# Gating a batch's loads behind the transpose ahead, reordering start-up PSUM banks, and turning q one step sooner

## The chip, the cores and the metric

The kernel runs on one core of one Trainium2 chip. The core has TensorE (PE, matmuls), VectorE (DVE), ScalarE (ACT), GpSimd (POOL) and SyncE (SP), each with its own stream of instructions, executed in order. SP and POOL issue most of the DMA transfers here. Matmul results go to PSUM, eight banks of 2 KB in each of 128 partitions; all else lives in SBUF. The metric is device time in microseconds for one execution; lower is better.

## The reference

A linear attention without softmax feeds a two-layer MLP. Eight batches, eight heads, 576 rows, head size 64; the MLP has 4608 tokens, width 512 and hidden width 2048. Its input is the attention's output, with the heads side by side.

```python
def _attn_ref(q, k, v, g_norm):
    kv = np.einsum('bhsd,bhse->bhde', k, v)
    out = np.einsum('bhsd,bhde->bhse', q, kv)
    rms = np.sqrt(np.mean(out * out, axis=-1, keepdims=True) + 1e-06)
    return (out / rms * g_norm).astype(np.float32)

def _moe_ref(x, w_in, w_out):
    h = x @ w_in
    g = np.where(h > 0.0, h, alpha * (np.exp(np.minimum(h, 0.0)) - 1.0))   # alpha = 1
    return (g @ w_out).astype(np.float32)
```

Inputs and output are float32; the kernel computes its matmuls in bfloat16.

## The kernel before

**Groups.** The 4608 tokens are worked in nine groups of 512. Group T below 8 holds the first 512 rows of batch T; group 8 holds the last 64 rows of all eight batches. Batch and group share their number. A group's MLP has eight steps. A step `mm1(T, i)` makes two 128-wide blocks of the hidden layer, transposed, with eight matmuls of 128x512 (line 399); ScalarE takes the exponential from PSUM (line 411), VectorE makes min(e, 1) - 1 (line 420) and the maximum of that and h (line 428), which gives `gT`. With `relu` ScalarE also writes relu(h) to SBUF (line 415) and VectorE adds that instead of reading PSUM. The second product `mm2` (line 444) gathers 16 matmuls for each of four output blocks `o_ps`, copied by ScalarE (line 457) and stored by SP (line 466). From group 2 on the second product of group T-1 runs between the steps of group T, and so does the attention of batch T+1.

**Attention of one batch.** Its pieces are, in order: `kv` (72 small matmuls, line 177, then ScalarE's copies into the block-diagonal `bd_kv`, line 356); `se` for two halves (line 208, from qT and bd_kv, then a square on ScalarE); sums, the reciprocal root, and VectorE's scaling into `xs` (line 242); and the turn of xs into `xT`. For batches 1 and 2 TensorE turns xs. From batch 3 on SP does it in two DMA transposes (`xd0`, `xd1`, line 327), and VectorE scales each half by g (`xg0`, `xg1`, line 334). In group T these pieces stand after steps 0 (kv), 1 (se0), 2 (xd0), 3 (se1), 4 (xd1), 5 (xg0) and 6 (xg1). Step 0 of the next group needs xT complete.

**Loads.** `fetch(b)` has POOL issue the loads of q, k and v of batch b, which cast float32 to bfloat16 on the way (lines 104 and 118), and then unpack q with four copies (line 151); the last of these stands behind a 1-element copy that waits for v (`gate<-v_pk`, line 125). When q is unpacked, SP issues a DMA transpose into `qT` (`qd`, line 265), in program order after the group's xT transposes and stores. `landed` is another 1-element POOL copy; it reads qT of a batch, and so holds back all that stands behind it on POOL until that transpose has landed. Before the change it stands ahead of the loads of batches 3 and 4 alone. k, v and q have two buffers each.

**Start.** Group 0 has its own code. Batch 0's q is turned by TensorE; kv, se, squares, means (a matmul with a matrix of 1/64), logarithm, exponential and scaling follow for the four head pairs c = 0 to 3 (`kv_first`, `se_first`, `square_first`, `mean_first`, `log_first`, `exp_first`, `scale_first`). They use banks by name; a name gets its place in PSUM in the order of first use, behind the two banks of `kv`. After `head.close()` the pools of the main part take the same eight banks: `at` the first two, then two h_ps tiles of two banks (`ps_m1`), then two single banks (`ps_m2`). A new tile waits for the last reader of what lay there. Idle matmuls on zeros (line 525) fill gaps.

**q of batch 1.** Batch 1's q is turned by TensorE, 32 transposes (`q_t`, line 188) into the tile `at`, during group 0; two copies bring it to SBUF (lines 258 and 259). kv of batch 1 uses `at` again, after step 7 of group 0, and the first quarter of the second product follows it.

Of the kernel before, what the change touches and what calls it, by code (L numbers as in the profile page):

```python
# [9 lines left out]
BF16 = mybir.dt.bfloat16  # L10
# [6 lines left out]
def kernel(  # L17
# [13 lines left out]
    nc = tc.nc  # L31
# [109 lines left out]
    def load_w_out(s):  # L141
        fs = slice(4 * s, 4 * s + 4)
        nc.gpsimd.dma_start(
            out=w_out_sb[:, fs, :], in_=moe_w_out.rearrange("(c p) f -> p c f", p=P)[:, fs, :]
        )
# [21 lines left out]
    def at_tile(dtype):  # L167
        full = ps_at.tile([P, 1024], FP32, name="at", tag="at")
        return full if dtype == FP32 else full.bitcast(BF16)
# [15 lines left out]
    def q_t_single(q_pk, qt_ps, p):  # L185
        for j in range(J):
            for l in range(2):
                nc.tensor.transpose(
                    qt_ps[l * 64 : l * 64 + 64, p, j * P : j * P + P],
                    q_pk[:, 2 * p + l, j, :],  # L190
                    ident,
                )
# [56 lines left out]
    def attention(T):  # L249
        st = {}  # L250

        def q_t():
            qt_ps = at_tile(BF16).rearrange("p (r t) -> p r t", r=NPAIR)
            qT = attp.tile([P, NPAIR, G], BF16, name="qT", tag="qT")
            st["qT"] = lambda p, j: qT[:, p, j * P : j * P + P]
            for p in range(NPAIR):
                q_t_single(raw["q", T], qt_ps, p)
            nc.vector.tensor_copy(out=qT[:, 0:2, :], in_=qt_ps[:, 0:2, :])
            nc.scalar.copy(qT[:, 2:4, :], qt_ps[:, 2:4, :])

        def q_dma():
# [99 lines left out]
        def kv_part(u):  # L361
# [4 lines left out]
            return product  # L366

        pieces = {"kv": kv_all, "q": q_t, "qd": q_dma}
        pieces["landed"] = lambda: after(st["at"])
        for h in range(2):  # L370
# [12 lines left out]
    def mm1(T, i, cols=(slice(0, 512),), relu=False, spare=False):  # L383

        if i == 0:
            gT[T] = mlpg.tile([P, FC, G], BF16, name="gT", tag="gT")
        x = xT[T]
        if spare:
            h_ps = [ps_m2.tile([P, G], FP32, name="h_ps", tag="mm2") for _ in range(2)]
            parts = [(a, a + 1, h_ps[a].rearrange("p (a t) -> p a t", a=1)) for a in range(2)]  # L390
        else:
            both = ps_m1.tile([P, 2, G], FP32, name="h_ps", tag="mm1")
            h_ps = [both[:, a, :] for a in range(2)]
            parts = [(0, 2, both)]
        for cs in cols:
            for a in range(2):
                f = 2 * i + a
                for c in range(KC):
                    nc.tensor.matmul(  # L399
                        h_ps[a][:, cs],  # L400
                        lhsT=w_in_sb[:, c, f * P : f * P + P],
                        rhs=x(c, cs),
                        start=(c == 0),
                        stop=(c == KC - 1),
                    )
        return elu(T, i, parts, relu)
# [32 lines left out]
    def mm2(T, j, f0, f1, hold=False):  # L439

        if f0 == 0 and (T, j) not in o_ps:
            o_ps[T, j] = ps_m2.tile([P, DM], FP32, name="o_ps", tag="mm2")
        for f in range(f0, f1):
            nc.tensor.matmul(  # L444
                o_ps[T, j],
                lhsT=gT[T][:, f, j * P : j * P + P],
                rhs=w_out_sb[:, f, :],
                start=(f == 0),
                stop=(f == FC - 1),
            )  # L450
        if f1 == FC and not hold:
            mm2_out(T, j)
# [50 lines left out]
    for s in range(2):  # L503
# [7 lines left out]
        out=g_row,  # L511
        in_=bass.AP(tensor=g_norm.tensor, offset=g_norm.offset, ap=[[1, 1], [0, 2], [1, 64]]),
# [7 lines left out]
    def bank(n):  # L520
        return ps_head.tile([P, G], FP32, name=f"bank{n}", tag=f"bank{n}")

    def idle(ps, n):
        for _ in range(n):
            nc.tensor.matmul(ps, lhsT=zeros[:, 0:P], rhs=zeros, start=True, stop=True)

    kv_ps = ps_head.tile([P, 2, G], FP32, name="kv_ps", tag="kv")
    idle_ps, g_ps = bank(2), bank(3)
    qt_ps = [bank(n).bitcast(BF16).rearrange("p (r t) -> p r t", r=2) for n in (4, 5, 1)]
    idle(idle_ps, 9)  # L530
    q_st = q_tile(0)
    qT0 = attp.tile([P, NPAIR, G], BF16, name="qT", tag="qT")
# [15 lines left out]
    xT[0] = lambda c, cs: x0[:, c, cs]  # L548
    sq0 = [attp.tile([P, G], BF16, name="sq0", tag="sq0", bufs=4) for _ in range(KC)]
    r0 = [attp.tile([P, G], FP32, name="r0", tag="r0", bufs=4) for _ in range(KC)]  # L550
    mean0 = {}

    def kv_first(c):
        u, l = c // 2, c % 2
# [4 lines left out]
    def se_first(c):  # L559
        u, l = c // 2, c % 2  # L560
        ls = slice(l * 64, l * 64 + 64)
        for s in range(2):
            nc.tensor.matmul(
                se0[c][s * 64 : s * 64 + 64, :],
                lhsT=kv0[ls, u, s, :],
                rhs=qT0[ls, 2 * s + u, :],
                start=True,
                stop=True,
            )

    def square_first(c, eng):
        if eng is A:
            nc.scalar.activation(sq0[c], se0[c], AF.Square)
        else:
            nc.vector.tensor_copy(out=r0[c], in_=se0[c])
            nc.vector.tensor_tensor(out=sq0[c], in0=r0[c], in1=se0[c], op=ALU.mult)

    def mean_first(c):
        nc.tensor.matmul(mean0[c], lhsT=means, rhs=sq0[c], start=True, stop=True)

    def log_first(c):
        nc.scalar.activation(r0[c], mean0[c], AF.Ln, bias=eps_col)  # L582

    def exp_first(c):
        nc.scalar.activation(r0[c], r0[c], AF.Exp, scale=-0.5)  # L585

    def scale_first(c):
# [13 lines left out]
        start=True,  # L601
# [5 lines left out]
    square_first(0, A)  # L607
    kv_first(1)
    idle_ps = bank(4)
    for c in range(2):  # L610
        mean0[c] = bank(2 + c)
    mean_first(0)
    log_first(0)
    se_first(1)
# [14 lines left out]
    idle_ps = bank(2)  # L629
    idle(idle_ps, 1)  # L630
    mean_b = ps_head.tile([P, 2, G], FP32, name="mean_ps", tag="kv")
    mean0[2] = mean_b[:, 0, :]
    mean_first(2)
    log_first(2)
    exp_first(2)
    se_first(3)
    square_first(3, V)
    scale_first(1)
    scale_first(2)
# [14 lines left out]
    for c in range(KC):  # L654
        for f in (2, 3, 0, 1) if c == 0 else range(4):
# [4 lines left out]
                start=(c == 0),  # L660
                stop=(c == KC - 1),
            )
    at, ahead = attention(1), attention(2)
    for i in range(2):
        elu(0, i, [(0, 2, firsts[i])], i == 0)()
    for i in range(2, 8):
        mm1(0, i, relu=i in (2, 4, 7), spare=i in (3, 6))()
        if i in (3, 5):
            load_w_out(i // 2)
        if i == 6:  # L670
            at["q"]()
    for l in range(2):
        ls = slice(l * 64, l * 64 + 64)
        nc.gpsimd.tensor_copy(
            out=bd_kv[ls, 0].rearrange("p (s u) e -> p u s e", s=2)[:, :, :, ls], in_=kv0[ls]
# [38 lines left out]
    def fetch(b):  # L714
        if b < B:
            fetch_packed_q(b)
            packed_kv(b)
            for name in "kv":
                fetch_packed_kv(name, b)
            unpack_q(b, Q)  # L720
        else:
            fetch_q(B)
            cast_q(B, Q)

    def group(T, at, start, second, relu=()):


        early, late = {}, {}
        for name, i in start.items():
            if name in ("se0", "se1"):  # L730
                early.setdefault(i + 1, []).extend(("sum" + name[2], "inv" + name[2]))
                late.setdefault(i + 1, []).insert(0, "mul" + name[2])
            late.setdefault(i, []).append(name)
        for i in range(9 if 8 in early else 8):
            if i == 8:
                for name in early[8] + late[8]:
                    at[name]()
                break
            rest = mm1(T, i, (slice(0, 512),), i in relu)
            for name in early.get(i, ()):  # L740
                at[name]()
            for piece in second.get(i, ()):
                mm2(*piece)
            rest()
            for name in late.get(i, ()):
                at[name]()
# [3 lines left out]
    at, ahead = ahead, attention(3)  # L750
# [22 lines left out]
    for T in range(2, NT):  # L773
        second = {i: [(T - 1, i // 2, 8 * (i % 2), 8 * (i % 2) + 8)] for i in range(8)}
        if T == 2:
            quarters = [(1, 2 + i // 4, 4 * (i % 4), 4 * (i % 4) + 4) for i in range(2, 8)]
            second = {i + 1: [piece] for i, piece in enumerate(quarters)}
        at, start = ahead, {}
        if T + 1 < NT:
            start = {"kv": 0, "se0": 1, "xd0": 2, "se1": 3, "xd1": 4, "xg0": 5, "xg1": 6}  # L780
        if T + 2 < NT:
            if T == 2:
                at["landed"]()
            fetch(T + 2)
            ahead = attention(T + 2)
        group(T, at, start, second)
        if T + 2 < NT:
            ahead["qd"]()
    rows = out.rearrange("(i l s) f -> l s i f", l=2, s=S)
# [2 lines left out]
    for j, cols in pieces:  # L792
        n = cols.stop - cols.start
        ps = ps_m2.tile([P, DM], FP32, name="o_ps", tag="mm2")[:, 0:n]
        for f in range(FC):
# [4 lines left out]
                start=(f == 0),  # L800
# [36 lines left out]
```

## Time and profile before

| | us |
|---|---|
| median of three runs (298.2, 300.46, 299.97) | 299.97 |
| the profiled execution's own time | 298.37 |
| its span, first to last instruction | 296.6 |
| PE busy | 279.1 (94%) |
| DVE busy | 171.6 (58%) |
| ACT busy | 139.7 (47%) |
| POOL busy | 52.2 (18%) |

The mean granted clock of TensorE was 0.987 of full speed. Matmuls of 128x512 are listed with a mean of 383 ns each but follow each other faster than that, since they overlap. The page's chain of work that ended last is 83% PE. DMA engines moved 35.96 MB, most of it in the first half.

In the lines below, a row of the timeline gives start, length, engine, line, operation, output and input, count, and in brackets the idle time before it with what ended it. A row of the waits gives the total, the number and the longest. A row of the chain gives start, length and what; "x8" counts instructions.

### The profile page before, as it was taken

The numbers are of one execution on the slowest core, as the hardware profiler recorded it, in microseconds if no ns is written. First come the engines' busy times: TensorE is split into PE (matmuls) and PEld (weight loads), VectorE is DVE, ScalarE is ACT, GpSimd is POOL, SyncE is SP. The second block draws the span as 40 slices with busy tenths as digits, with TensorE's granted clock in tenths as the row PEclk, the third lists the DMA queues.
The fourth block names the chain that finished last, engine by engine and source line by source line (L and its number), as shares of the span: only waits on it lengthen the run. The fifth ranks groups of instructions, "written<-read, shape, count | busy, mean of one in ns | idle before, by whom it ended". The sixth has DMA issues, their size and how long they took to land.

```text
span 296.6 us, 4818 instructions
## 1 busy us (share of the span) xinstructions
PE 279.1 (94%) x1971; PEld 134.8 (45%) x2001; DVE 171.6 (58%) x221; ACT 139.7 (47%) x201; POOL 52.2 (18%) x90
## 2 busy tenths in 40 slices
PE   6889699999999499999999999999999999999995
PEld 2444345445544144444444444444444444444444
DVE  5449551678398428754875477547765776544400
ACT  3768444774465125543554455345534554334311
POOL 7726103423245222202100000001200000000000
PEclk9999999999999879999999999999999999999999
DMA  7999996993979969926931506164545031101122
GB/s 196 206 204 204 207 204 114 258 185 74 197 117 174 260 75 155 166 49 147 156 106 35 145 0 108 35 161 96 135 38 141 5 105 34 71 11 62 66 76 71
DMA packets 55961, 35.96 MB, mean 121 GB/s; under 512 B 32772, under 2 KB 53508, under 8 KB 55940
## 3 DMA queue, kind: packets, MB, share of 16 engines
q0 software_dynamic: 20192, 17.30, 37.7%
q1 hardware_dynamic: 35348, 17.83, 23.6%
q10 hardware_dynamic: 400, 0.52, 0.5%
q8 instruction: 15, 0.25, 0.3%
q14 instruction: 6, 0.05, 0.1%
HBM read 36.70 MB, written 9.44 MB: 156 GB/s over the span
## 4 chain that ended last, share of the span: by engine, by line
PE 83%; DVE 6%; DMA 4%; ACT 4%; issue 1%; SPq 0%; DVEq 0%
PE h_ps L399 36%; PE o_ps L444 35%; PE o_ps L796 5%; DVE gT L428 3%; DMA xT<-xs 2%; PE at L208 2%; DMA st_q<-in_q_dram 2%; PE at L177 2%; ACT elu_e L411 2%; DVE elu_e L420 1%; DVE xs L242 1%; PE h_ps L656 1%; ACT r L582 1%; PE at L306 0%; ACT r L585 0%
## 5 line engine op out<-in xcount | busy, mean ns | idle before, releaser
L399 PE MATMUL h_ps<-xT,w_in_sb 128*128 128x512 bf16 x555 | 132.3, 383 | 4.6 <-DVE xT L334 4.3
L444 PE MATMUL o_ps<-w_out_sb,gT 128*128 128x512 bf16 x490 | 118.8, 382 | 1.3 <-issue 0.2
L411 ACT ACTIVATE elu_e<-h_ps 128x1024 bf16<-128x1024 f32 (+1 forms) x75 | 72.9, 981 | 92.7 <-PE h_ps L399 90.4
L399 PEld LDWEIGHTS <-w_in_sb 128*128 128x128 bf16 x560 | 53.9, 99 | 67.3 <-DVE xT L334 4.8
L428 DVE TENSOR_TENSOR gT<-elu_e,h_ps 128x1024 bf16<-128x1024 bf16 (+1 forms) x69 | 80.0, 1159 | 7.2
L444 PEld LDWEIGHTS <-gT 128*128 128x128 bf16 x512 | 50.3, 99 | 60.2 <-issue 2.2
L420 DVE TENSOR_SCALAR elu_e<-elu_e 128x1024 bf16<-128x1024 bf16 (+1 forms) x76 | 32.8, 431 | 76.0 <-ACT elu_e L411 76.0
L457 ACT COPY o_sb<-o_ps 128x512 f32<-128x512 f32 x32 | 18.5, 585 | 21.1 <-PE o_ps L444 21.1
L232 DVE TENSOR_REDUCE ss<-sq 128x16 f32<-128x1024 bf16 x16 | 19.3, 1217 | 8.0 <-ACT sq L227 7.9
L151 POOL COPY q_bf<-q_pk 128x512 bf16<-128x512 bf16 x24 | 14.5, 634 | 22.8 <-DMA q_pk<-in_q_dram 22.8
L242 DVE TENSOR_TENSOR xs<-at,ss 128x1024 bf16<-128x1024 f32 x14 | 17.0, 1216 | 0.0
L227 ACT ACTIVATE sq<-at 128x1024 bf16<-128x1024 f32 x14 | 14.4, 1027 | 2.0 <-PE at L208 2.0
L796 PE MATMUL o_ps<-w_out_sb,gT 128*128 128x512 bf16 (+1 forms) x79 | 14.0, 336 | 0.1
L118 POOL DMA_DIRECT2D k_pk<-in_k_dram x12 | 8.3, 695 | 30.3 <-PE at L177 24.6
L151 POOL CAST q_bf<-st_q 128x512 bf16<-128x512 f32 x4 | 2.7, 680 | 59.1 <-DMA st_q<-in_q_dram 59.1
L104 POOL DMA_DIRECT2D q_pk<-in_q_dram x14 | 10.5, 754 | 2.3 <-DMA v_pk<-in_v_dram 0.7
L796 PEld LDWEIGHTS <-gT 128*128 128x128 bf16 x80 | 7.8, 98 | 6.3
L356 ACT CAST bd_kv<-at 64x256 bf16<-64x256 f32 (+1 forms) x16 | 5.4, 338 | 9.8 <-PE at L177 9.7
L177 PEld LDWEIGHTS <-k_pk 64*64 64x64 bf16 x576 | 6.8, 107 | 6.4 <-issue 6.1
L208 PEld LDWEIGHTS <-qT 128*128 128x128 bf16 x112 | 7.3, 98 | 4.2 <-issue 1.3
L118 POOL DMA_DIRECT2D v_pk<-in_v_dram x12 | 8.3, 690 | 2.2 <-DMA w_in_sb<-in_moe_w_in_dram 1.8
L208 PE MATMUL at<-bd_kv,qT 128*128 128x128 bf16 x96 | 7.3, 219 | 1.2 <-ACT bd_kv L356 0.6
(71 smaller groups left out, 109.0 us busy)
## 6 DMA issues: line engine op xcount, KB each, us to landing
out_dram<-o_sb SPq DMA_DIRECT2D x16, 512.0 KB, 3.0
q_pk<-in_q_dram POOLq DMA_DIRECT2D x14, 256.0 KB, 5.2
k_pk<-in_k_dram POOLq DMA_DIRECT2D x6, 576.0 KB, 7.8
v_pk<-in_v_dram POOLq DMA_DIRECT2D x6, 576.0 KB, 10.2
w_in_sb<-in_moe_w_in_dram POOLq DMA_DIRECT2D x4, 512.0 KB, 10.9
w_out_sb<-in_moe_w_out_dram POOLq DMA_DIRECT2D x4, 512.0 KB, 14.9
st_q<-in_q_dram SPq DMA_DIRECT2D x2, 512.0 KB, 4.6
st_q<-in_q_dram SPq DMA_DIRECT2D x16, 64.0 KB, 2.4
```

Of the source, the lines that this page charges most:

```text
L118: nc.gpsimd.dma_start(out=raw[name, b].rearrange("p h j d -> p h (j d)")[:, hs], in_=in_[:, hs])
L151: eng.tensor_copy(out=out_, in_=in_)
L208: nc.tensor.matmul(ov[:, u, :, s, :], lhsT=qT(p, j), rhs=bd_kv[:, T, p, :], start=True, stop=True,)
L232: nc.vector.reduce_sum(out=ss, in_=sq.rearrange("p c (h e) -> p (c h) e", h=H), axis=AX.X)
L242: nc.vector.tensor_tensor(out=xs.rearrange("p c (h e) -> p (c h) e", h=H), in0=se_ps.rearrange("p c (h e) -> p (c h) e", h=H), in1=ss.to_b ...
L399: nc.tensor.matmul(h_ps[a][:, cs], lhsT=w_in_sb[:, c, f * P : f * P + P], rhs=x(c, cs), start=(c == 0), stop=(c == KC - 1),)
L411: nc.scalar.activation(e[:, lo:hi, :], ps, AF.Exp)
L420: nc.vector.tensor_scalar(out=e[:, lo:hi, :], in0=e[:, lo:hi, :], scalar1=1.0, scalar2=1.0, op0=ALU.min, op1=ALU.subtract,)
L428: nc.vector.tensor_tensor(out=gT[T][:, 2 * i + lo : 2 * i + hi, :], in0=e[:, lo:hi, :], in1=h, op=ALU.add if relu else ALU.max,)
L444: nc.tensor.matmul(o_ps[T, j], lhsT=gT[T][:, f, j * P : j * P + P], rhs=w_out_sb[:, f, :], start=(f == 0), stop=(f == FC - 1),)
L457: nc.scalar.copy(o_sb[T][:, j % 2, :], o_ps.pop((T, j)))
L796: nc.tensor.matmul(ps, lhsT=gT[B][:, f, j * P : j * P + P], rhs=w_out_sb[:, f, cols], start=(f == 0), stop=(f == FC - 1),)
```

## The change

There are five edits.

1. **The gate.** `landed` stands ahead of every `fetch(T + 2)`, for T = 2 to 6, and not only at T = 2. So the loads of batches 5, 6 and 7 wait until qT of batches 4, 5 and 6 has landed; at T = 6 the casts of the last group's q stand behind it (its loads are on SP).
2. **Banks of group 0.** The idle matmuls start on bank 0, q's third turned piece is given bank 1 by name at the start, g's column gets bank 2, and bank 3 is for the mean of c = 1 alone until the mean of c = 3 takes it. The order of first use becomes 0, 1, 2, 3, 4, 5 where it was 2, 3, 4, 5, 1, 0.
3. **se_first(3)** stands ahead of the mean of c = 2 and no longer behind it.
4. **q of batch 1** is turned after step 5 of group 0 and no longer after step 6, and both copies are ScalarE's.
5. **ReLU in group 2.** Steps 1 and 2 of group 2 use the ReLU form.

```diff
-            nc.vector.tensor_copy(out=qT[:, 0:2, :], in_=qt_ps[:, 0:2, :])
+            nc.scalar.copy(qT[:, 0:2, :], qt_ps[:, 0:2, :])
             nc.scalar.copy(qT[:, 2:4, :], qt_ps[:, 2:4, :])
...
     kv_ps = ps_head.tile([P, 2, G], FP32, name="kv_ps", tag="kv")
-    idle_ps, g_ps = bank(2), bank(3)
-    qt_ps = [bank(n).bitcast(BF16).rearrange("p (r t) -> p r t", r=2) for n in (4, 5, 1)]
+    idle_ps, qt_b, g_ps = bank(0), bank(1), bank(2)
+    mean0 = {1: bank(3)}
+    qt_ps = [
+        t.bitcast(BF16).rearrange("p (r t) -> p r t", r=2) for t in (bank(4), bank(5), qt_b)
+    ]
...
-    mean0 = {}
...
-    for c in range(2):
-        mean0[c] = bank(2 + c)
+    mean0[0] = bank(2)
     mean_first(0)
...
     mean0[2] = mean_b[:, 0, :]
+    se_first(3)
     mean_first(2)
     log_first(2)
     exp_first(2)
-    se_first(3)
     square_first(3, V)
...
-        if i == 6:
+        if i == 5:
             at["q"]()
...
         if T + 2 < NT:
-            if T == 2:
-                at["landed"]()
+            at["landed"]()
             fetch(T + 2)
             ahead = attention(T + 2)
-        group(T, at, start, second)
+        group(T, at, start, second, (1, 2) if T == 2 else ())
```

**The gate on POOL**, at the end of batch 4's unpacking and the start of batch 5's loads (the same piece occurs for batches 6 and 7). `gate<-qT` is the copy that waits for qT of batch 4:

```order
 L125 COPY gate<-v_pk 1x1
 L151 COPY q_bf<-q_pk 128x512
+L125 COPY gate<-qT 1x1
 L104 DMA q_pk<-in_q_dram 128x4x256 x2
 L118 DMA k_pk<-in_k_dram 128x4x576
```

The loads of q and k, which stood directly behind the unpacking, now stand behind a copy that reads qT.

**ScalarE in group 0**, from the ReLU of step 4 to the ReLU of step 7. `elu_e<-h_ps 128x512 x2` is step 6, whose two blocks lie in single banks; L258 and L259 are the two halves of qT of batch 1:

```order
 L415 ACTIVATE elu_h<-h_ps 128x1024
 L411 ACTIVATE elu_e<-h_ps 128x1024
+L258 COPY qT<-at 128x1024
+L259 COPY qT<-at 128x1024
 L411 ACTIVATE elu_e<-h_ps 128x512 x2
-L259 COPY qT<-at 128x1024
 L411 ACTIVATE elu_e<-h_ps 128x1024
 L415 ACTIVATE elu_h<-h_ps 128x1024
```

One copy came over from VectorE, and both stand ahead of step 6's exponentials and no longer behind them.

**TensorE in the head**, between the last kv_first and the idle matmuls, first as it was. kv_ is the copied kv product (kv0 in the code), bank_265 holds the se product of c = 3, and mean_ps the mean of c = 2:

```order
L579 LDWEIGHTS means
L579 MATMUL mean_ps<-sq_171,means 128x512
L563 LDWEIGHTS kv_167
L563 MATMUL bank_265<-qT,kv_167 64x512
L563 LDWEIGHTS kv_167
L563 MATMUL bank_265<-qT,kv_167 64x512
```

And as it is now (lines counted in the changed file):

```order
L565 LDWEIGHTS kv_168
L565 MATMUL bank_265<-qT,kv_168 64x512
L565 LDWEIGHTS kv_168
L565 MATMUL bank_265<-qT,kv_168 64x512
L581 LDWEIGHTS means
L581 MATMUL mean_ps<-sq_172,means 128x512
```

The two matmuls of se for c = 3 went ahead of the mean of c = 2; the idle matmuls behind them are as before.

## The prediction

> **What bounds the kernel now.** I read the page first (shares, 40 slices), then who waited for whom, then the chain that ended last, and last the timeline of POOL and SP around the one weak place. Page:
> ```profile
> span 296.6 us, 4818 instructions
> PE   6889699999999499999999999999999999999995
> PEclk9999999999999879999999999999999999999999
> ```
> TensorE is full from about the fifth slice on (a slice is 7.4 us), so only its gaps are worth something: slices 1 to 6, and the 4 in slice 14, behind which the granted clock dips. The waits of PE name these gaps (total, times, longest):
> ```profile
> PE h_ps L399 <- DVE xT L334: 4.3, 1, 4.3
> PE at L177 <- ACT qT L259: 2.6, 1, 2.6
> ...
> PE h_ps L656 <- ACT r L582: 0.6, 1, 0.6
> ```
> The chain shows the first one in place (start, us, what):
> ```profile
> 93.93 7.30 DMA xT<-xs
> 101.25 0.50 DVE xT L334
> 101.80 3.60 PE h_ps L399 x8
> ...
> 108.36 0.71 PE at L177 x72
> ...
> 134.24 1.73 PE h_ps L399 x8
> ...
> 137.69 0.84 PE at L177 x72
> ```
> Group 3 begins with the first-product matmuls at 101.80. They waited for DVE's scaling of the second half of batch 3's xT, and that for a DMA transpose of 7.30 us. Then eight matmuls take 3.60 us; the same eight take 1.73 one group later. The reader sees two losses: an idle stretch and a slow stretch behind it. Why the transpose was slow stands on POOL's timeline, the median landings beside it:
> ```profile
> 72.68 1.49 POOL L104 DMA_DIRECT2D q_pk<-in_q_dram  x2 [0.28 <-issue]
> ...
> 87.67 0.60 POOL L151 COPY q_bf<-q_pk 128x512 bf16<-128x512 bf16 x1
> 88.22 1.49 POOL L104 DMA_DIRECT2D q_pk<-in_q_dram  x2
> ...
> 100.66 0.18 POOL L125 COPY gate<-v_pk 1x1 bf16<-1x1 bf16 x1 [4.63 <-DMA v_pk<-in_v_dram]
> ```
> ```profile
> xT<-xs SPq DMA_TRANSPOSE x12, 3.3
> qT<-q_bf SPq DMA_TRANSPOSE x7, 4.4
> ```
> POOL issued batch 5's casting loads at 88.22, right after batch 4's q was unpacked. They were in flight until v landed at 100.66. The transpose (93.93 to 101.23) lay inside that and took 7.3 instead of the usual 3.3 us.
>
> **The gate (the main part).** It adds four 1-element POOL copies; the one that matters stands ahead of batch 5's loads. It waits for qT of batch 4, whose transpose SP issues after both xT transposes of batch 3 and a store. Those two stand in one row (start of the first, and the stretch to the issue of the second):
> ```profile
> 87.42 7.75 SPq L327 DMA_TRANSPOSE xT<-xs  x2
> ```
> So the new loads can't start before both xT halves have been issued, and the stretch from 88.22 on is free of loads. What is late next? The tail of group 2:
> ```profile
> 95.62 1.89 PE L399 MATMUL h_ps<-xT,w_in_sb 128*128 128x512 bf16 x8
> 96.75 1.22 DVE L428 TENSOR_TENSOR gT<-elu_e,h_ps 128x1024 bf16<-128x1024 bf16 x1
> ```
> PE is through at 97.5. With 3.3 us the transpose lands at 97.2; DVE is busy until 97.97 and then takes 0.5 for the scaling, so it is ready at about 98.2 to 98.5. I leave a stall of 0.7 to 1.0, and take 0.7, since two DVE operations just ahead lay beside POOL's work on the loads that now move. From 97.5 to the next kv product at 108.36 went 10.86 us for work that takes 137.69 - 134.24 = 3.45 in the next group: 7.4 lost. With 0.7 left, the gain is 6.7, if the clock stays up; bounds 0 (the transpose stays slow) and 7.4. Does a short gap drop the clock? Two windows (us, busy PE, PEld, DVE, ACT, POOL, clock, DMA, GB/s):
> ```profile
> 31.00:33.60 2.60, 0.07 (x1) 0.10 (x1) 1.42 (x3) 1.04 (x2) 1.48 (x2) 1.00 1.22 208
> 101.80:104.00 2.20, 2.20 (x6) 0.83 (x7) 1.50 (x2) 0.00 (x0) 1.50 (x2) 0.50 1.31 247
> ```
> After 4.3 us of idleness the clock is 0.50; through the 2.6 us of idleness in group 0 it stayed 1.00. So 0.7 us should leave it up.
>
> What is queued behind the gate? POOL's loads and unpacking, nothing else; who needs those: q's transpose at the end of the same group, and kv in the next. In groups 3 to 5 the gate opens when qT lands, 4.4 us after its issue, and the full set of loads with unpacking took 88.27 - 72.68 = 15.6 us, together 20 (with the 7.3 of a disturbed transpose, 23). A group lasts 137.69 - 108.36 = 29.3. The cover is 6 to 9 us; cost 0. The loads now also lie beside the first xT transpose of groups 3 to 5. For that the trace has a case, batch 4's, issued beside loads:
> ```profile
> 118.84 1.23 SPq L327 DMA_TRANSPOSE xT<-xs  x1
> ...
> 126.15 1.23 SPq L327 DMA_TRANSPOSE xT<-xs  x1
> ...
> DMA to landing us min/median/max: 7.0/7.0/7.0
> ...
> 128.36 0.48 DVE L334 TENSOR_SCALAR xT<-xT,g_col 128x1024 bf16<-128x1024 bf16 x1
> ```
> The first half landed 7.0 us after its issue (the landing row is that of 118.84) and DVE came for it only after 9.5, without a wait. Cover 2.5 us, cost 0. The second half is issued 7.3 us after the first, when the loads are in.
>
> The Trainium skill (DMA: Bandwidth & Descriptors, section Rules for kernel authors) says to issue a transfer early, compute, and wait late. That speaks against this gate, which starts batch 5's loads some 10 us later. No row here shows a late start costing anything, and by the cover above the sum keeps its value; by the rule alone the gate would be a loss, and that is the slower rival below. The same page (section Issuing engines are not separate DMA queues) has the transfers of all queues interleave on the same 16 engines: the loads then must collide with some transpose, and the question is only whether with one that has cover; the two xT cases above agree.
>
> **The head.** Bank 3 held the last mean, and the first h_ps tile lay on it, so PE waited for ScalarE's logarithm (the 0.6 above). In the new allocation order the first h_ps tile lies on the banks of se0 0 and 1, which VectorE frees by its second scaling. PE then has 14 matmuls of 0.216 (1.73 / 8) left without a gap. Their last four need the last scaling; rows:
> ```profile
> 12.99 0.10 PEld L579 LDWEIGHTS <-means 128*128 128x128 bf16 x1 [0.61 <-DVE kv L557]
> 13.31 0.11 PEld L563 LDWEIGHTS <-kv 64*64 64x64 bf16 x2 [0.23 <-issue]
> ...
> 17.04 0.75 DVE L588 SCALAR_TENSOR_TENSOR xT<-bank,g_col,r 128x512 bf16<-128x512 f32 x1 [0.55 <-ACT r L585]
> ```
> se_first(3) ahead of the mean goes out 13.31 - 12.99 = 0.3 earlier and brings the last scaling from 17.79 to 17.5; the last four matmuls start at about 18. So -0.6; bounds 0 and -0.9.
>
> **q of group 1.** Today VectorE's copy of qT comes behind its backlog, ScalarE's waits for it, and kv of batch 1 waits for both:
> ```profile
> 31.84 0.68 DVE L258 COPY qT<-at 128x1024 bf16<-128x1024 bf16 x1
> 32.56 1.01 ACT L259 COPY qT<-at 128x1024 bf16<-128x1024 bf16 x1 [3.71 <-DVE qT L258]
> ```
> One step sooner and both on ScalarE they run behind the exponential of step 5, from about 27 to 29 (2 x 1.01), and kv starts when step 7's matmuls end: -2.6. The price is that step 6's exponentials come 2 us later; their products come out on VectorE behind step 5's as now, and what they free is wanted only after kv and eight matmuls. Cost 0; bounds 0 and -2.6. Together the early part would be 3.2 earlier. What could be late next are loads whose time PE doesn't set:
> ```profile
> 20.60 0.71 POOL L118 DMA_DIRECT2D v_pk<-in_v_dram  x1 [1.82 <-DMA w_in_sb<-in_moe_w_in_dram]
> ...
> DMA to landing us min/median/max: 13.7/13.7/13.7
> ...
> 23.14 0.74 POOL L143 DMA_DIRECT2D w_out_sb<-in_moe_w_out_dram  x1 [1.83 <-DMA w_in_sb<-in_moe_w_in_dram]
> ...
> DMA to landing us min/median/max: 13.2/13.2/13.2
> ...
> 37.59 0.48 PE L177 MATMUL at<-v_pk,k_pk 64*64 64x64 bf16 x36
> ```
> The second half of v of batch 1 lands at 34.3, w_out's second quarter at 36.3. kv's second half moves from 37.59 to 34.4, and the second quarter of o_ps, which follows some 2 us behind it with ScalarE's copies and the se products between, starts at about 36.5. Both loads arrive just ahead of their use. I take 2.8 of the 3.2, for a sliver of either wait; bounds 0 and 3.2.
>
> **ReLU in group 2, steps 1 and 2.** It adds two ScalarE passes and shortens two VectorE products (mean ns behind the count):
> ```profile
> L428 DVE TENSOR_TENSOR gT<-elu_e,h_ps 128x1024 bf16<-128x1024 bf16 x61 | 74.5, 1221 | 6.4
> L415 ACT ACTIVATE elu_h<-h_ps 128x1024 bf16<-128x1024 f32 x6 | 6.2, 1027 | 0.0
> L428 DVE TENSOR_TENSOR gT<-elu_e,elu_h 128x1024 bf16<-128x1024 bf16 x6 | 4.5, 756 | 2.1 <-ACT elu_h L415 1.9
> ```
> +2.1 us on ScalarE, -0.9 on VectorE. But each product now starts behind a ReLU that is a microsecond later than the exponential, and the reciprocal roots queue behind the second one. So the first scaling of batch 3 comes out at the same time. 0; bounds -0.5 and +0.5.
>
> **Sum.** The profiled execution took 298.37 (span 296.6 and 1.77 around it): 298.37 - 2.8 - 6.7 = 288.9, given as 289.0. It stands 1.6 below the median of the runs shown, 299.97. I don't add that: the runs may differ by just the stall that goes. It stays in the upper end.
>
> **Rivals.**
> - Early gain eaten by the loads: PE arrives earlier, v and w_out don't. For it: the margins of about 0.2 us; against: no PE wait for a load anywhere today. 298.37 - 6.7 = 291.7.
> - The clock falls all the same: the 0.7 us gap, or a somewhat longer one, drops it to 0.50, and sixteen matmuls cost 3 us more: 292.0. Against: the 2.6 us gap without a drop.
> - The stall stays, since PE now comes 2.8 us earlier to transposes while batch 4's loads keep their time: the first xT half of batch 3 is then issued at 87.42 - 2.8 = 84.6, beside loads that are in and unpacked only at 88.27, and the second, behind it on the same queue, may be late too; or the gate opens too soon and does nothing. 298.37 - 2.8 = 295.6. Against: the second half goes out at 93.93 - 2.8 = 91.1, after the last load, and the order of instructions has the gate ahead of the loads.
> - Slower: late loads. Each of the gates for batches 5, 6 and 7 delays a set of loads; if loading and unpacking took more than 29.3 - 4.4 = 25 us instead of 15.6, q of the next batch would be late in each of three groups. It decides from 28 us on, where 3 x (28.2 - 25) eats the whole gain of 9.5; at 30 us it is 288.9 + 3 x 5 = 304. Against: nearly twice the measured set would be needed.
>
> **How the numbers follow.** Forecast 0.66, eaten early gain 0.12, clock 0.08, stall stays 0.10, slower 0.04. The time is the forecast's, 289.0, its own range 287.0 (all of 3.2 and 7.4, and a little from the ReLUs) to 291. The first two rivals end at 292.0, and with the 1.6 by which the median stood above the profiled execution, at 293.5; the range 287.0 to 293.5 leaves out the last two rivals. A measurement of this kernel tells about 1% from no change, so faster means below 297.0: the first four cases but for a part of the fourth whose runs also lie high, 0.92; within 1% 0.05; slower 0.03.
>
> **What would show it.** Right: batch 5's first load at about 99 (xT at 91.1, a store, then qT at about 94 and 4.4 to land), behind a gate copy that waited for qT; the xT transpose issued at about 91 landing in 3 to 4 us; PE's gap ahead of group 3 under 1 us and clock 1.00 in the slice; ScalarE's two qT copies ending before 29.5 and kv of batch 1 starting at about 30.5; no PE wait for a load. Wrong: a PE wait for w_out or v near 34 to 37, a clock under 1.00 near 95, DVE waiting for an xT transpose in groups 3 to 5, or SP's qT transposes waiting for POOL late in a group.

## The result, and the profile after

| | us |
|---|---|
| median of four runs before (298.2 to 300.46) | 299.88 |
| median of four runs after (288.57 to 288.75) | 288.71 |
| ratio, with its 95% interval | 0.963 (0.960 to 0.967) |
| profiled execution after, its own time / span | 288.75 / 286.7 |

The kernel is 11.2 us faster by the medians, and 9.6 us by the two profiled executions, on which the sum was made. Some executions take over 1.5% longer than the fastest of the same kernel, at a lower granted clock; all medians and ranges here and below are without them. The page of the changed kernel, with TensorE's row and the granted clock in 40 slices:

```profile
span 286.7 us, 4859 instructions
PE   7899899999999999999999999999999999999994
PEclk9999999999999999999999999999999999999999
```

The 4 in slice 14 and the dip of the clock behind it are gone, and the early slices are fuller. Of the waits of PE (total, times, longest) these are left at the places of the prediction:

```profile
PE h_ps L399 <- DVE xT L334: 0.7, 1, 0.7
...
PE o_ps L444 <- DMA w_out_sb<-in_moe_w_out_dram: 0.3, 1, 0.3
```

The 4.3 us for xT are 0.7, the 2.6 us for qT and the 0.6 us for ScalarE's r are gone, and a wait of 0.3 us for the second product's weights (their first quarter) is new. The chain that ended last, at the start of group 3 (start, us, what):

```profile
92.71 0.44 DVE elu_e L420
93.24 1.22 DVE gT L428
94.46 0.41 DVE xT L334
94.92 1.90 PE h_ps L399 x8
96.82 1.73 PE o_ps L444 x8
98.55 0.71 PE at L177 x72
```

No transfer is in it any more. The scaling of xT stands behind VectorE's own queue (gT ends when it starts), and the eight matmuls of the second product take 1.73 us, so the clock holds. The timeline of POOL and SP shows the gate at work:

```profile
93.62 2.56 SPq L265 DMA_TRANSPOSE qT<-q_bf  x1
...
98.20 0.18 POOL L125 COPY gate<-qT 1x1 bf16<-1x1 bf16 x1 [12.66 <-DMA qT<-q_bf]
98.65 1.49 POOL L104 DMA_DIRECT2D q_pk<-in_q_dram  x2 [0.27 <-issue]
...
110.80 0.18 POOL L125 COPY gate<-v_pk 1x1 bf16<-1x1 bf16 x1 [4.42 <-DMA v_pk<-in_v_dram]
```

POOL stood still for 12.66 us until qT of batch 4 was in, and issued batch 5's loads at 98.65 (forecast: about 99). Their last one, v, was in at 110.80, 17 us before the kv product of batch 5 at 127.81. The early part, from the timeline of PE and ACT:

```profile
26.70 1.01 ACT L258 COPY qT<-at 128x1024 bf16<-128x1024 bf16 x1
27.61 1.02 ACT L259 COPY qT<-at 128x1024 bf16<-128x1024 bf16 x1
30.15 0.48 PE L177 MATMUL at<-v_pk,k_pk 64*64 64x64 bf16 x36
30.88 3.63 PE L444 MATMUL o_ps<-w_out_sb,gT 128*128 128x512 bf16 x16 [0.26 <-DMA w_out_sb<-in_moe_w_out_dram]
34.44 0.48 PE L177 MATMUL at<-v_pk,k_pk 64*64 64x64 bf16 x36
```

Both copies end at 28.63, and the second half of batch 1's kv starts at 34.44 where it started at 37.59.

A kv product (line 177) stands near the start of each group, so its starts, read from the same timeline, say in which stretch time was won. The two halves of batch 1, then batches 2 to 7:

| kernel | 1a | 1b | 2 | 3 | 4 | 5 | 6 | 7 |
|---|---|---|---|---|---|---|---|---|
| before | 33.63 | 37.59 | 57.86 | 77.72 | 108.29 | 137.62 | 167.08 | 196.54 |
| after | 30.15 | 34.44 | 54.71 | 74.57 | 98.48 | 127.81 | 157.26 | 186.70 |

Up to 1b 3.15 us are won, from batch 3 to batch 4 another 6.66 (30.57 becomes 23.91), and nothing anywhere else.

### The profile page after: what moved, and what is told of

Same layout as the page of the kernel before. It is cut to its first block, busy times and chain, and to the rows that moved or that the text cites. A ratio compares the mean times of both kernels' runs of the same rounds, so it can differ in the third digit from the quotient of the medians.

```text
span 286.7 us, 4859 instructions
## 1 busy us (share of the span) xinstructions
PE 278.5 (97%) x2001; PEld 134.2 (47%) x2001; DVE 169.4 (59%) x220; ACT 142.2 (50%) x204; POOL 53.2 (19%) x94
## 3 DMA queue, kind: packets, MB, share of 16 engines
HBM read 36.70 MB, written 9.44 MB: 161 GB/s over the span
## 4 chain that ended last, share of the span: by engine, by line
PE 86%; DMA 10%; DVE 1%; ACT 1%; issue 1%; DVEq 0%; POOLq 0%
PE h_ps L399 38%; PE o_ps L444 38%; DMA w_out_sb<-in_moe_w_out_dram 6%; PE o_ps L796 5%; DMA w_in_sb<-in_moe_w_in_dram 3%; PE at L208 2%; DMA k_pk<-in_k_dram 2%; PE at L177 2%; PE at L306 0%; DVE xs L242 0%; DVE gT L428 0%; PE at L217 0%; ACT elu_e L411 0%; PE se_ps L208 0%; ACT bd_kv L356 0%
## 5 line engine op out<-in xcount | busy, mean ns | idle before, releaser
L399 PE MATMUL h_ps<-xT,w_in_sb 128*128 128x512 bf16 x560 | 130.9, 379 | 0.7 <-DVE xT L334 0.7
L444 PE MATMUL o_ps<-w_out_sb,gT 128*128 128x512 bf16 x512 | 120.5, 379 | 0.3 <-DMA w_out_sb<-in_moe_w_out_dram 0.3
L428 DVE TENSOR_TENSOR gT<-elu_e,h_ps 128x1024 bf16<-128x1024 bf16 (+1 forms) x67 | 77.5, 1157 | 7.0
L125 POOL COPY gate<-qT 1x1 bf16<-1x1 bf16 x6 | 1.1, 182 | 68.2 <-DMA qT<-q_bf 68.2
L525 PE MATMUL bank<-zeros 128*128 128x512 bf16 x19 | 7.3, 518 | 1.2 <-DVE zeros L500 1.2
```

What stands on the lines that cost most here:

```text
L399: nc.tensor.matmul(h_ps[a][:, cs], lhsT=w_in_sb[:, c, f * P : f * P + P], rhs=x(c, cs), start=(c == 0), stop=(c == KC - 1),)
L428: nc.vector.tensor_tensor(out=gT[T][:, 2 * i + lo : 2 * i + hi, :], in0=e[:, lo:hi, :], in1=h, op=ALU.add if relu else ALU.max,)
L444: nc.tensor.matmul(o_ps[T, j], lhsT=gT[T][:, f, j * P : j * P + P], rhs=w_out_sb[:, f, :], start=(f == 0), stop=(f == FC - 1),)
```

## The experiments

Each stood beside runs of the kernel before on the same chip (medians 299.1, 299.2 and 298.7 on three chips).

**The changed kernel without the new gates.** Theory: the gate is worth about 7 us and nothing else in the change touches that stall.

```diff
-            at["landed"]()
+            if T == 2:
+                at["landed"]()
```

> All edits of the change but the gate: the loads of batches 5 to 7 go out as before. Theory (the gate removes the stall ahead of group 3): batch 5's loads are issued at about 85.5, the second xT transpose of batch 3 at about 90.4 lies beside them and lands after about 7 us, PE waits some 4 us ahead of group 3 and runs the next sixteen matmuls at half clock: 294.5 to 296.5. Rival (the gate is worth nothing, the early part and the ReLUs brought it all): 288.5 to 289.5, the gap ahead of group 3 under 1 us.

It took 296.42 (295.60 to 296.97), 0.991 (0.988 to 0.994). In its timeline and windows (window, busy PE, PEld, DVE, ACT, POOL, clock, DMA, GB/s):

```profile
86.29 1.49 POOL L104 DMA_DIRECT2D q_pk<-in_q_dram  x2
...
99.69 0.56 DVE L334 TENSOR_SCALAR xT<-xT,g_col 128x1024 bf16<-128x1024 bf16 x1 [4.58 <-DMA xT<-xs]
100.30 3.59 PE L399 MATMUL h_ps<-xT,w_in_sb 128*128 128x512 bf16 x8 [5.87 <-DVE xT L334]
```
```profile
100.00:102.00 2.00, 1.70 (x5) 0.60 (x6) 1.80 (x3) 0.00 (x0) 1.45 (x2) 0.50 1.21 289
```

The loads go out ungated again, at 86.29. PE waits 5.87 us, longer than before: it is through with the work ahead 3.1 us sooner (94.4, 97.5 before), while the loads go out only 1.9 us sooner (88.22 before). The clock is 0.50 behind the wait. The early part alone ends up as 31.52 us from batch 3 to 4, so it loses a microsecond of its own gain in this stall. By the medians the gate is worth 7.7 us in the changed kernel (296.42 - 288.71). A rule of the Trainium skill points the other way: DMA: Bandwidth & Descriptors, section Rules for kernel authors, says to issue a transfer early, compute, and wait late. Here the earlier issue, with more cover than it needed, is the slower one.

**The kernel before with all gates, and nothing else.**

```diff
-            if T == 2:
-                at["landed"]()
+            at["landed"]()
```

> The kernel before with the gate alone. Theory: the gap ahead of group 3 shrinks from 4.3 to about 0.7 to 1.0 us, clock 1.00 behind it: 6.5 us off the profiled execution, 291.5 to 293.5. Rival (late loads cost what the gate brings): 297 or more.

292.73 (292.0 to 294.49), 0.981 (0.976 to 0.987). From batch 3 to 4 it takes 24.06 us. Its waits of PE:

```profile
PE at L177 <- ACT qT L259: 2.6, 1, 2.6
...
PE h_ps L399 <- DVE xT L334: 0.7, 1, 0.7
```

The gates alone bring 6.4 us by the medians of this chip (299.1 - 292.73), and leave 0.7 us at the same place; the early part is left as it was.

**The kernel before with the gate of batch 5 only.** The prediction held that this gate is the one that matters.

```diff
-            if T == 2:
+            if T in (2, 3):
                 at["landed"]()
```

> The kernel before with the gate ahead of batch 5's loads alone; batches 6 and 7 load as before. Theory (only this gate matters, the others cost and bring nothing): as the run with all gates, within 0.5 us: 291.5 to 293.5. Rival 1 (the later gates also save something): a microsecond or more slower than with all gates. Rival 2 (the later gates cost): a microsecond or more faster than with all gates.

294.96 (294.48 to 296.42), 0.988 (0.983 to 0.993): 2.2 us behind all gates on the same chip. From batch 3 to 4 it takes 24.05 us, as with all of them, but from batch 4 to 5 31.63 where 29.3 is usual, 2.3 us more. Chain and timeline there:

```profile
120.70 9.54 DMA xT<-xs
```
```profile
116.91 1.60 POOL L104 DMA_DIRECT2D q_pk<-in_q_dram  x2 [0.60 <-issue]
...
129.84 0.18 POOL L125 COPY gate<-v_pk 1x1 bf16<-1x1 bf16 x1 [5.42 <-DMA v_pk<-in_v_dram]
...
130.27 0.58 DVE L334 TENSOR_SCALAR xT<-xT,g_col 128x1024 bf16<-128x1024 bf16 x1 [3.83 <-DMA xT<-xs]
130.91 1.90 PE L399 MATMUL h_ps<-xT,w_in_sb 128*128 128x512 bf16 x8 [2.13 <-DVE xT L334]
```

The stall has moved one group on. Batch 5's loads are later now, so batch 6's, without a gate, go out at 116.91 and lie beside the second transpose of batch 4's xs: 9.54 us. The rival was right: the gates of batches 6 and 7 are needed because of that of batch 5.

**What the low clock costs: the kernel before with twenty idle matmuls put into the stall.** They go to a tile that nobody reads.

```diff
+        if T == 3:
+            idle(at_tile(FP32)[:, 0:512], 20)
         group(T, at, start, second)
```

> The kernel before with 20 idle matmuls on zeros put ahead of group 3's first step, where PE waits 4.3 us; the wait itself stays. Theory (the slow stretch behind the wait is TensorE's clock, which falls because PE is idle): the clock stays 1.00, the sixteen matmuls behind the wait take 3.5 us and not 6.6, the time falls by about 3 us to 295.3 to 297. Rival (the slow stretch comes from the DMA traffic beside it, or from waits that the trace doesn't show): the matmuls stay slow and the time stays at 298 to 300.5.

296.62 (295.35 to 297.43), 0.990 (0.984 to 0.996). Timeline and window:

```profile
103.64 1.90 PE L399 MATMUL h_ps<-xT,w_in_sb 128*128 128x512 bf16 x8
105.38 1.89 PE L444 MATMUL o_ps<-w_out_sb,gT 128*128 128x512 bf16 x8
107.19 0.78 PE L177 MATMUL at<-v_pk,k_pk 64*64 64x64 bf16 x72
```
```profile
103.60:106.00 2.40, 2.36 (x11) 1.09 (x12) 1.54 (x2) 0.42 (x1) 1.50 (x2) 1.00 1.28 242
```

With TensorE kept busy, the clock stays at 1.00 and the sixteen matmuls take 3.55 us (103.64 to 107.19) where they took 6.56, though the DMA engines carry as much (1.28 beside 1.31 before). That rules out the loads as the cause of the slow matmuls. So about 3 us of the 7.4 lost were the clock, and the rest the wait. The medians differ by 2.5 us (299.1 - 296.62).

**q of batch 1 as before, the rest of the change in place.**

```diff
-            nc.scalar.copy(qT[:, 0:2, :], qt_ps[:, 0:2, :])
+            nc.vector.tensor_copy(out=qT[:, 0:2, :], in_=qt_ps[:, 0:2, :])
...
-        if i == 5:
+        if i == 6:
             at["q"]()
```

> The changed kernel with q of batch 1 turned after step 6 again and its first copy on VectorE. Theory (kv of batch 1 waits for the copies): PE waits some 2.5 us for ScalarE's copy of qT; the 0.26 us that the changed kernel waits for w_out goes: 2.3 us slower than the changed kernel's 288.7, 290.5 to 291.5. Rival (loads limit the early part anyway): under 289.3.

293.09 (293.11, 293.07, 290.87, 293.24), 0.977 (0.971 to 0.983). Only the run at 290.87 is where theory had it. The profiled one is at 293.11:

```profile
33.23 0.48 PE L177 MATMUL at<-v_pk,k_pk 64*64 64x64 bf16 x36 [2.69 <-ACT qT L259]
```
```profile
31.00:33.00 2.00, 0.00 (x0) 0.00 (x0) 1.13 (x2) 0.84 (x1) 1.07 (x2) 1.00 1.21 207
34.00:35.00 1.00, 0.78 (x3) 0.41 (x3) 0.43 (x1) 1.00 (x3) 0.00 (x0) 0.50 1.23 203
35.00:36.00 1.00, 1.00 (x4) 0.34 (x3) 0.69 (x1) 0.41 (x3) 0.00 (x0) 0.50 1.26 210
```

A gap of 2.69 us, and the clock is 0.50 behind it; the two kv halves are 5.64 us apart (33.23, 38.87) instead of 4.0 to 4.3. In the profile of before, a gap of 2.6 us at the same place left the clock at 1.00; the last section has this gap in all five profiles that show it.

**The same, with that gap filled by eleven idle matmuls** into a tile that is written later.

```diff
-    at["kv0"]()
     both = ps_m1.tile([P, 2, G], FP32, name="o_ps", tag="mm1")
+    idle(both[:, 0, :], 11)
+    at["kv0"]()
```

> As the run with q turned as before, with 11 idle matmuls on zeros in the gap of 2.7 us ahead of batch 1's kv. Theory (that gap lets the clock fall in some executions, which cost 2.2 us there): no run at 293, all within 290.6 to 291.3, clock 1.00 between 33 and 36. Rival (the two groups of run times have another cause): runs at 293 remain as often as before, 3 of 4.

291.8 (291.95, 291.35, 291.65, 293.37), 0.977 (0.970 to 0.983). In the profile:

```profile
33.17 0.48 PE L177 MATMUL at<-v_pk,k_pk 64*64 64x64 bf16 x36 [0.27 <-ACT qT L259]
```
```profile
34.00:35.00 1.00, 1.00 (x6) 0.49 (x5) 0.43 (x2) 1.00 (x3) 0.00 (x0) 1.00 1.23 204
```

kv starts as late as in the last kernel, the clock is 1.00, and the halves are 3.97 apart. That fits a clock that falls because the gap is empty, but one profile doesn't show it: of the five with the gap empty, three kept 1.00 too. By the runs, one of four is at 293 where it was three of four. The total is half a microsecond above what was expected. The cause is likely, not shown.

**q one step sooner, its first copy on VectorE.**

```diff
-            nc.scalar.copy(qT[:, 0:2, :], qt_ps[:, 0:2, :])
+            nc.vector.tensor_copy(out=qT[:, 0:2, :], in_=qt_ps[:, 0:2, :])
```

> The changed kernel with q turned after step 5, but the first copy on VectorE as before. Theory (one step sooner is most of it; VectorE's copy stands behind step 5's products and holds ScalarE's copy and step 6's exponentials back by 1 to 2 us): 0.2 to 0.8 us slower, 288.9 to 289.5. Rival (the move to ScalarE is what counts): 2 us or more slower, 290.7 or more.

291.11 (290.90, 288.72, 291.39, 291.32), 0.970 (0.964 to 0.976). Timeline and window:

```profile
30.95 0.68 DVE L258 COPY qT<-at 128x1024 bf16<-128x1024 bf16 x1
31.67 1.01 ACT L259 COPY qT<-at 128x1024 bf16<-128x1024 bf16 x1 [3.50 <-DVE qT L258]
32.73 0.48 PE L177 MATMUL at<-v_pk,k_pk 64*64 64x64 bf16 x36 [1.15 <-ACT qT L259]
```
```profile
8.00:12.00 4.00, 3.12 (x65) 2.01 (x60) 1.07 (x4) 2.64 (x5) 4.00 (x6) 0.75 1.22 204
```

VectorE comes to its copy only at 30.95, hardly sooner than the 31.84 of before, and PE waits 1.15 us. So moving the turn without moving the copy keeps a part of the wait. This execution also ran at 0.75 in its first microseconds. The profile of the last kernel of this section has the same dip (0.74), and its kv halves start at 31.45 and 35.41; against that, this kernel's (32.73 and 36.70) are 1.3 us late. The median lies where the rival had it. What the copy costs in all stays open, since the best run, 288.72, is as fast as the changed kernel.

**Without the ReLUs of group 2** (`group(T, at, start, second)`).

> The changed kernel without the ReLU form in steps 1 and 2 of group 2. Theory (neutral): within 0.5 us of 288.7, and the wait of the second se product for VectorE's scaling 0.1 to 0.2 us longer. Rival (VectorE's 0.9 us less work is what keeps the gap ahead of group 3 at 0.7): the gap grows to 1.5 us or more, 289.5 or more.

288.85 (288.72 to 290.89), 0.967 (0.960 to 0.973), and 0.7 us of waiting ahead of group 3, as with them. They do nothing that these runs can tell.

**With the old head**: the old order of banks, and se_first(3) behind the mean again.

> The changed kernel with the bank order and the order of se and mean of the kernel before. Theory: the first exponential of group 0 starts 0.8 us later, of which the wait for w_out's first quarter swallows 0.3: 0.5 to 0.6 us slower, 289.1 to 289.5. Rival (loads limit the early part): no change, 288.5 to 288.9.

289.01 (288.86 to 290.96), 0.966 (0.961 to 0.972): 0.3 us behind the changed kernel, between theory and rival and less than runs of one kernel tell apart. Its batch 1 kv halves start at 31.02 and 34.99: the 0.87 us that the new head is ahead at the first half is 0.55 at the second. The banks and the order of se and mean were not tried apart.

**The loads later still.** The loads of batches 5 to 7 are issued behind a copy that reads the second half of the next xT.

```diff
+        pieces["x_ap"] = lambda: st["x"][0:1, 2, 0, 0:1]
...
-            at["landed"]()
-            fetch(T + 2)
+            if T in (2, 6):
+                at["landed"]()
+                fetch(T + 2)
             ahead = attention(T + 2)
...
+            if T in (3, 4, 5):
+                after(at["x_ap"]())
+                fetch(T + 2)
             ahead["qd"]()
```

> The loads of batches 5 to 7 wait for more: for the landing of the second xT half of the batch ahead, some 19 us later in the group. Theory (the gate costs nothing only because 15.6 us of loading and unpacking fit into the rest of the group): q's transpose comes some 7 us late for its se product in groups 4 to 6, with the clock falling in each stall: 21 to 33 us slower, 310 to 322. Rival (late loads hardly matter): under 292.

323.41 (two runs, 323.2 and 323.61), 1.082 (1.071 to 1.092), a microsecond above what was expected. Waits, timeline and window:

```profile
PE at L177 <- DMA v_pk<-in_v_dram: 28.0, 3, 9.7
```
```profile
123.03 0.18 POOL L125 COPY gate<-xT 1x1 bf16<-1x1 bf16 x1 [36.27 <-DVE xT L334]
137.40 1.18 PE L177 MATMUL at<-v_pk,k_pk 64*64 64x64 bf16 x72 [9.10 <-DMA v_pk<-in_v_dram]
```
```profile
137.40:140.00 2.60, 2.60 (x76) 1.62 (x76) 0.00 (x0) 0.73 (x2) 0.72 (x2) 0.50 0.26 60
```

The gate opens at 123.03 instead of 98.20, 24.8 us later, and v had 17 us to spare: 24.8 - 17 = 7.8, and PE waits 9.10; without that wait this product would start at 128.30, close to the 127.81 of the changed kernel. From batch 4 on the kv products stand 38.5, 41.3 and 40.6 us apart instead of 29.3 to 29.5; the three waits make 28.0 us of it, and the clock is 0.50 behind each. What PE waits for is v, for kv, and not q, as the prediction's slower rival and this experiment's theory had it.

**The changed kernel again**, on the chip of the last two kernels and of the next.

> The changed kernel once more, on the chip of the next three, to see how much its own runs differ there. Theory (no gap in it is long enough to let the clock fall after step 5 of group 0): all runs at 288.5 to 289.0. Rival (the clock also falls in the start-up of some executions): some runs 2 us longer, at 290.5 to 291.5, with a mean clock of 0.99.

288.77 (288.50, 291.11, 288.71, 288.83), 0.967 (0.960 to 0.975). One run of four is 2.4 us longer, at a mean granted clock of 0.988 against 0.997 to 1.000 in the others.

**The scaling of xT moved ahead.** In group 2 VectorE scales the second half of batch 3's xT ahead of the last product and no longer behind it, and step 6 uses the ReLU form too.

```diff
+            if T == 2 and i == 6:
+                at["xg1"]()
             rest()
             for name in late.get(i, ()):
-                at[name]()
+                if (T, name) != (2, "xg1"):
+                    at[name]()
...
-        group(T, at, start, second, (1, 2) if T == 2 else ())
+        group(T, at, start, second, (1, 2, 6) if T == 2 else ())
```

> The changed kernel with VectorE's scaling of the second xT half ahead of step 6's products in group 2, and step 6 in the ReLU form so that its PSUM tile is freed by ScalarE. Theory (the 0.7 us left ahead of group 3 is VectorE's, the transpose lands about a microsecond earlier): the gap falls to 0.1 to 0.3, 288.1 to 288.5. Rival (the transpose is late too, or step 6's products make the next step wait): no gain, 288.6 or more.

288.15 (287.75 to 288.70), 0.963 (0.956 to 0.970). Timeline:

```profile
93.30 3.66 PE L399 MATMUL h_ps<-xT,w_in_sb 128*128 128x512 bf16 x16
94.48 0.49 DVE L334 TENSOR_SCALAR xT<-xT,g_col 128x1024 bf16<-128x1024 bf16 x1 [1.03 <-DMA xT<-xs]
```

Sixteen matmuls run without a gap, and from batch 3 to 4 it takes 23.06 us instead of 23.91. By the median it is 0.6 us ahead of the changed kernel on the same chip, about the size of the gap; the ranges overlap from 288.50 to 288.70. It is the fastest of all kernels here.

## Why the prediction was right, and where it was not

Both terms of the sum came out for the profiled executions: 2.8 was taken for the early part and 3.15 measured, 6.7 for the gate and 6.66 measured. The total gain between them is 9.6 us (298.37 - 288.75), where 9.4 was forecast.

- **The gate.** The mechanism is shown from both sides: without the gates the stall is back (5.87 us), with the gates alone it is gone. The 0.7 us that stay behind VectorE's queue are there to a tenth, and removing them brought about 0.6. That two fifths of the price of the stall were the clock, for which the prediction had only the two durations 3.60 and 1.73, is shown by the idle matmuls.
- **"The one that matters stands ahead of batch 5's loads": this failed.** The prediction gave the other gates no gain: in the profile of before, batch 4's transposes have cover beside loads. That cover belonged to the old times of the loads. With batch 5's loads moved, batch 6's come beside the second half's transpose, and 2.13 us of waiting and 2.3 us in all return. The total was right only because the change has all gates.
- **The early part.** Its size came out better than its parts. The head was taken at 0.6, and the first exponential came 0.84 sooner (18.34, 19.18 before); q's wait of 2.56 is gone; 0.26 went to a wait for w_out: 0.84 + 2.56 - 0.26 = 3.14. The sign "no PE wait for a load" failed, at a place that the prediction had not named: it watched w_out's second quarter, which was in at 36.4 and used at 36.45 without a wait. PE waited for the first quarter, issued at 14.52 and in 16.3 us later, at 30.8. Of the two terms q's is the one that pays: undoing it moved the second kv half by 4.4 us in the profiled execution, undoing the head by 0.55. In the total the head comes to 0.3, within the noise.
- **"The 2.6 us idle left the clock up": this was no rule.** In two of the four other profiles with a gap at that place, of 2.56 and 2.69 us, it fell to 0.50. So q's turn was priced as a wait of 2.6 us; against the changed kernel's 288.71 it is worth 4.4 in the profiled execution (293.11), and 2.2 in the best one (290.87), which has no profile. The clock rival was rejected with an argument that doesn't carry. Its rejection held all the same: ten profiles have the gap of 0.7 us ahead of group 3, and in each the sixteen matmuls behind it take 3.56 us.
- **ReLU** at 0 within 0.5: 288.85 without it.
- **Slower by late loads** was rejected for the right reason, cover, but the cover that ends first is v's 17 us and not that of q's transpose. Past it the kernel lost 9 to 12 us in each group.
- The medians lie 1.6 us further apart than the two profiled executions. The profiled execution of before was 1.5 under its median; the runs after lie within 0.2 us. Before has both gaps behind which the clock can fall, and the changed kernel neither, which would explain its narrower runs; the one at 291.11 says that it is not all. This was not settled.

## What to carry to other kernels

A small transpose that the next matmuls wait for can be worth more than the early start of large loads: hold the loads back until it is through, as long as they keep cover, and work that cover out for each consumer of the load. Hold back every such load and not only the one that is seen to collide, since a load that moves can make the next one collide. Price an idle stretch on TensorE with the slow matmuls behind it, and don't take one execution in which the clock stayed up for a rule.

## What the runs showed of the hardware

- **Short gaps and the clock.** Five profiles have q of batch 1 as before and leave the gap ahead of its kv empty:

  | kernel | idle, us | 1a to 1b, us | clock behind the gap |
  |---|---|---|---|
  | before | 2.56 | 3.96 | 1.00 |
  | before, with all gates | 2.56 | 3.96 | 1.00 |
  | before, with the gate of batch 5 | 3.23 | 3.97 | 1.00 |
  | before, with idle matmuls in the stall | 2.56 | 5.30 | 0.50 |
  | changed, with q as before | 2.69 | 5.64 | 0.50 |

  The length of the gap doesn't decide between them, and what does is open. The Trainium skill (TensorE: Matmul & The Clock Gate, section HAM oscillation — how this bites in real kernels) asks for no idle gap of TensorE above about 3.4 us. By that none of these should count; the measurement decides, and a gap of 2.6 us can be enough.
- **A clock that differs from run to run.** Runs of the changed kernel, and of five of its variants, fall into two groups about 2 us apart; the longer ones have a mean clock of 0.988 to 0.994, the others 0.997 to 1.000. Two profiles, of the kernel with q one step sooner and of the one with the scaling moved, show a dip in the start-up: 0.75 and 0.74 from 8 to 12 us, while PE was busy for 3.12 and 3.59 of 4 us. In the second of them kv of batch 1 starts about a microsecond later than in the profiles of the changed kernel (31.45, against 30.15 and 30.41). What chooses the group is open.
- **The transpose beside casting loads.** In the changed kernel a half of xT lands 3.0 to 4.4 us after its issue in most groups, but after 6.3 and 8.1 us where loads are in flight beside it for nearly all of that time, and after 9.54 us in the kernel with the gate of batch 5 only. In this last one it ended at 130.24, when v had just landed (129.84). The 8.1 us are these:

```profile
167.92 1.46 SPq L327 DMA_TRANSPOSE xT<-xs  x1
...
DMA to landing us min/median/max: 8.1/8.1/8.1
...
177.57 0.48 DVE L334 TENSOR_SCALAR xT<-xT,g_col 128x1024 bf16<-128x1024 bf16 x1
```

This is group 5 of the changed kernel. VectorE comes for it 9.65 us after the issue, so here the 8.1 us cost nothing; the margin is 1.5 us.
